# Casts of q and k with the heads outermost, four of them joined, and a new order of the first quarter of an attention-and-MLP kernel

## The chip, the core and the metric

The kernel runs on one core of a Trainium2 chip. A core has five engines that run beside each other, each with its own instruction queue taken strictly in the order in which the kernel wrote it: TensorE (PE in the profile; PEld is its weight load), VectorE (DVE), ScalarE (ACT), GpSimd (POOL) and SyncE (SP, which issues DMA transfers). An engine waits on semaphores for the others, and while it waits everything behind the waiting instruction in its queue waits too. The metric is the device time of one execution in microseconds (us), median of several runs.

## The reference

Four batches, eight heads, 768 positions, head size 64. Three of the heads are "retrieval" heads (0, 2, 6) with plain causal attention; the other five are "streaming" heads that see 4 sink positions and a window of 64. The attention output, 3072 tokens of 512, then goes through a two-layer MLP with a gate, 512 to 2048 to 512.

```python
scores = scale * np.matmul(q, k.transpose(0, 1, 3, 2))
full_mask = causal                        # retrieval heads
stream_mask = causal & (is_sink | in_win) # streaming heads
a = softmax(where(mask, scores, -1e9))
x = (a @ v).transpose(0, 2, 1, 3).reshape(B * S, H * D)
h = x @ w_in
g = h * (1 / (1 + exp(-beta * h)))
return g @ w_out
```

## The kernel before

**Tiling.** The 768 positions of a batch are two halves of 384, so there are 8 chunks (batch, half). A chunk has 4 units, each a pair of heads that share one 128-row tile; there are 32 units. The first two chunks, units 0 to 7, are the "first quarter".

**What a unit of the first quarter needs.** `load_qk` (line 107) loads q and k of a chunk as float32 in two groups `s0` and `s1` of four heads: units 0 and 1 read the one, units 2 and 3 the other. `cast` (240) turns one unit's q or k into bfloat16 (`qkb`, 128 rows by 384). `transpose_qk` (317) lets PE transpose it, three 128-column products into a PSUM bank `mm`, and `copy_qk` (325) brings it back to SBUF as `KT` or `QTD`. `sinks_of` (302) copies the keys that streaming heads use twice (`KO`). A unit's scores come as two tiles, 0 and 1. For each, `begin` (411) adds the mask with a product of an identity (line 422; unit 5 is masked afterwards on DVE instead, by `mask`, 472), `rows` (425) multiplies queries by keys (line 451) and `soft` (454) takes the exponential on ACT, 128 by 768 or 128 by 512 (line 460). The score tile `sp` has two buffers, so a third tile begins only when the first has been read by its exponential. `steps_PV` (515) multiplies by the values (line 532), `normalize` (538) divides on DVE, and for each pair of units `steps_X` (563) transposes the result with six products (line 570), which `copy_x` (578) copies to `xT`.

**The MLP.** `steps_G1` (592) makes 16 tiles `fi` of a chunk's hidden layer, four products of 384 columns each (line 600), a tanh on ACT (605) and a gate on DVE (608). `steps_G2` (624) is the second layer (line 653) and the output. A G1 tile of chunk 0 needs `xT` of both pairs of units and its quarter of `w_in`, which `load_w_in` (138) brings through POOL's DMA queue, as `load_w_out` (142) brings `w_out`.

**What sets the order.** Everything is recorded in a list written by hand. `RAMP` (785) covers units 0 to 7, `PLAN` (803) the other 24 units; each word is one step, and `do` (697) turns it into instructions. The order of the words gives each engine its own order; words for different engines don't wait for each other but for their data. The words that matter here, with `u` a unit and `i` a tile:

- `cku`, `cqu` casts of k and q, with the engine as last letter (`v` DVE, `a` ACT, `g` POOL); `tku`, `tqu` the transposes; `kku`, `kqu` the copies back; `kou` the sink keys.
- `adu.i`, `qku.i`, `exu.i` the mask product, the scores and the exponential; `pvu` two of the six parts of a unit's value product; `nou` the division; `mau.i` the mask of unit 5.
- `xxg`, `cxg` the transposes of a pair's output and its copy.
- `lvc.t`, `lqc.g` loads of v and of q and k, `win`, `won` of the weights, `cvc.t` the cast of v, `voc` copies of sink values. A `g` behind a load holds it back until POOL has reached that place.
- `zzn` issues n products of zeros, 512 columns each, whose result nobody reads (`keep_busy`, 510); nine more come at the very start (`idle`, 164).
- `mm`, `mA`, `mb` the next step of the MLP, `hm` and `hf` the two halves of a first G1 tile.

From `PLAN` on, PE always has MLP work to put between the steps of attention.

Of the kernel before, what the change touches and what calls it, by code (L numbers as in the profile page):

```python
# [10 lines left out]
F32 = mybir.dt.float32  # L11
# [7 lines left out]
def kernel(  # L19
# [13 lines left out]
    nc = tc.nc  # L33
# [68 lines left out]

    staged = {}
# [125 lines left out]
    def masks_late(h2):  # L231

        m = Mh[h2]
        if h2 == 0:
            return [lambda: nc.vector.tensor_copy(out=m[:, 3:5], in_=m[:, 1:3])]
        return [lambda i=i: nc.vector.tensor_copy(out=m[:, i:i + 2 * HT - 1:2], in_=Mh[0][:, i + 1:i + 2].to_broadcast([128, HT, 128]))
                for i in range(2)]


    def cast(u, name, copy):  # L240
        b, h2, p = units[u]
        c = u // NPAIR
        s = st_u.setdefault(u, {})
        if "qkb" not in s:
            s["qkb"] = att.tile([128, 2, HT, 2, D], BF16, name="qkb", bufs=4)
        copy(out=s["qkb"][:, "qk".index(name)], in_=staged[name, c, p // 2][:, p % 2:4:2].rearrange("p h t d -> p t h d"))
# [40 lines left out]
    def transposes_dma(c, names=("k", "q")):  # L287
# [10 lines left out]
        for u in range(c * NPAIR, (c + 1) * NPAIR):  # L298
            p = u % NPAIR
            st_u[u] = {"QT": QT[:, place[p], :]}  # L300

    def sinks_of(u):
# [12 lines left out]
        copy(out=ko[:, ka - 1:kz - 1, 0:64], in_=kt[:, None, 0:64].to_broadcast([128, n, 64]))  # L315

    def transpose_qk(u, name):

        s = st_u.setdefault(u, {})
        tp = ps_m.tile([128, 512], F32, name="mm").bitcast(BF16)[:, 0:HALF].rearrange("p (t j) -> p t j", t=HT)  # L320
        for t in range(HT):
            nc.tensor.transpose(tp[:, t, :], s["qkb"][:, "qk".index(name), t].rearrange("p h d -> p (h d)"), ident)  # L322
# [59 lines left out]
    def steps_QK(u):  # L382
# [89 lines left out]
        def mask(i):  # L472
            ev = views[i]
            ms = [[x for x, e in enumerate(tiles[i][r]) if e[5] is not None] for r in range(2)]
            if ms[0] and ms[0] == ms[1]:
                n = len(ms[0])
                m0 = tiles[i][0][0][5]
                nc.vector.tensor_mul(ev[:, :, 0:n], ev[:, :, 0:n], Mh[h2][:, None, m0:m0 + n].to_broadcast([128, 2, n, 128]))  # L478
            else:
                for r in range(2):  # L480
                    if ms[r]:
                        n = len(set(tiles[i][r][x][5] for x in ms[r]))
                        m0 = tiles[i][r][0][5]
# [213 lines left out]
    def do(word):  # L697
# [2 lines left out]
        n, i = int(n or 0), int(i or 0)  # L700
        if what in ("ck", "cq"):
            cast(n, what[1], copies[eng])
        elif what in ("tk", "tq"):
            step((170, lambda: transpose_qk(n, what[1])))
        elif what in ("kk", "kq"):
# [3 lines left out]
        elif what in ("ad", "qk", "ex", "ma"):  # L709
            if n not in visits:  # L710
                visits[n] = steps_QK(n)
            step((0 if what in ("ex", "ma") else 170, lambda: visits[n][what](i)))
        elif what == "cv":
            cast_v(n, i, copies[eng])
        elif what == "vo":
# [1 line left out]
        elif what == "pv":  # L717
            pv = products.setdefault(n, [])
            if not pv:
                pv.extend(steps_PV(n))  # L720
            run(pv[:2])
            del pv[:2]
        elif what == "no":
            normalize(n)
        elif what == "xd":
            x_by_dma(n)
        elif what == "xx":
            run(steps_X(n))
        elif what == "cx":
            copy_x(n, copies[eng])  # L730
        elif what == "on":
            ones_v(engines[eng], n)
        elif what == "ne":
            negatives([(0, 1, 2), (3, 4)][n])
        elif what == "be":
            step((100, beta_go))
        elif what == "lv":
            load_v(n, held=eng == "g", tiles=[i])
        elif what == "lq":
            load_qk(n, i, held=eng == "g")  # L740
        elif what == "wi":
            load_w_in(n)
        elif what == "wo":
            load_w_out(n)
        elif what == "rq":
            rows_queries()
        elif what == "rk":
            rows_keys()
        elif what == "ro":
            if n not in more_rows:  # L750
                more_rows[n] = load_rows(n)
            more_rows[n].pop(0)()
        elif what in ("dk", "dq"):
            transposes_dma(n, what[1])
        elif what == "ml":
            late[n].pop(0)()
# [12 lines left out]

    def feed(x):  # L770
# [141 lines left out]
```

## Time and profile before

| What | Value |
|---|---|
| median of 3 runs | 228.81 us (228.60 to 228.89) |
| profiled execution: span from first to last instruction | 227.0 us |
| what the median has beside that span | 1.8 us |
| PE busy | 219.4 us, 97% of the span |
| ACT busy | 154.0 us, 68% |
| DVE busy | 142.1 us, 63% |
| POOL busy | 87.3 us, 38% |
| mean granted TensorE clock | 0.999 |

No time of the profiled execution other than its span is given, so the median stands for it; the 1.8 us lie before the first and after the last instruction. In rows of the timeline the first number is the start in us from the start of the span, the second the length from the first start to the last end of a group of `x` instructions; then engine, line, operation, and output `<-` input. In brackets stands the idle time of the engine before the group, and what ended it. A product's row holds its latency too, so the next product starts before the row ends. "Busy" PE counts the products of zeros like any other.

### The profile page before, as it was taken

How to read it: one execution, taken by the hardware profiler on the slowest of the kernel's cores; microseconds unless marked ns; L12 is line 12 of the kernel's file. 1: busy time of each engine (PE TensorE's matmuls, PEld its weight loads, DVE VectorE, ACT ScalarE, POOL GpSimd, SP SyncE). 2: the span in 40 equal slices, each digit the busy share in tenths (PEclk: the TensorE clock that was granted, in tenths of full speed). 3: DMA queues.
4: the chain of work that ended last, by engine and by line, in shares of the span. 5: the costliest groups of instructions: out<-in, count | busy, mean ns of one | idle time of the engine just before them, and what ended most of it. 6: DMA issues, size and time to landing. Idle time of an engine off the chain costs nothing.

```text
span 227.0 us, 5019 instructions
## 1 busy us (share of the span) xinstructions
PE 219.4 (97%) x1898; PEld 126.4 (56%) x1917; DVE 142.1 (63%) x342; ACT 154.0 (68%) x254; POOL 87.3 (38%) x143
## 2 busy tenths in 40 slices
PE   7989999999999999999999999999999999999994
PEld 3555766654655665556654664556645655456553
DVE  4679888852684779357932699646963779028600
ACT  2698898946767897449933887569876878139621
POOL 5377952249163399143064049910670000000000
PEclk9999999999999999999999999999999999999999
DMA  6999999999999899989869779596963030111012
GB/s 204 262 301 239 225 197 198 195 220 171 149 216 178 161 153 144 141 175 133 103 131 162 126 151 140 92 133 103 216 64 107 24 81 0 49 46 46 0 49 92
DMA packets 95383, 31.66 MB, mean 139 GB/s; under 512 B 81776, under 2 KB 92416, under 8 KB 95360
## 3 DMA queue, kind: packets, MB, share of 16 engines
q1 hardware_dynamic: 58880, 22.82, 50.2%
q0 software_dynamic: 35904, 8.13, 41.9%
q10 hardware_dynamic: 576, 0.40, 0.6%
q8 instruction: 15, 0.25, 0.5%
q14 instruction: 8, 0.07, 0.1%
HBM read 27.27 MB, written 6.29 MB: 148 GB/s over the span
## 4 chain that ended last, share of the span: by engine, by line
PE 89%; DMA 4%; DVE 2%; SPq 2%; issue 1%; ACT 0%; ACTq 0%; DVEq 0%
PE mm L653 34%; PE mm L600 25%; PE sp L600 12%; PE sp L451 6%; PE po L532 6%; DMA s<-in_k_dram 3%; DMA s<-in_q_dram 2%; PE mm L638 2%; DVE es L478 1%; PE mm L322 1%; SPq L132 1%; PE mm L570 1%; PE mm L451 1%; SPq L119 1%; PE sp L422 1%
## 5 line engine op out<-in xcount | busy, mean ns | idle before, releaser
L653 PE MATMUL mm<-w_out_sb,gT 128*128 128x512 bf16 x349 | 84.1, 379 | 1.3 <-issue 0.5
L460 ACT ACTIVATE es<-sp 128x768 bf16<-128x768 f32 (+2 forms) x72 | 56.5, 837 | 19.6 <-PE sp L451 19.4
L600 PE MATMUL mm<-xT,w_in_sb 128*128 128x384 bf16 x348 | 64.6, 326 | 0.0
L600 PEld LDWEIGHTS <-w_in_sb 128*128 128x128 bf16 x512 | 47.8, 98 | 29.7 <-issue 0.2
L605 ACT ACTIVATE th<-mm,beta_h 128x384 f32<-128x384 f32 x87 | 49.8, 588 | 5.6 <-PE mm L600 0.9
L653 PEld LDWEIGHTS <-gT 128*128 128x128 bf16 x368 | 33.4, 98 | 36.0 <-issue 1.5
L608 DVE SCALAR_TENSOR_TENSOR gT<-th,mm 128x384 bf16<-128x384 f32 x87 | 46.8, 551 | 7.4 <-ACT th L605 3.8
L282 POOL DMA_DIRECT2D s<-in_q_dram x30 | 22.4, 761 | 27.2 <-DMA QTD<-s 21.7
L600 PE MATMUL sp<-xT,w_in_sb 128*128 128x384 bf16 x164 | 32.3, 326 | 0.0
L657 ACT ACTIVATE osb<-mm 128x512 f32<-128x512 f32 x23 | 13.8, 602 | 26.1 <-PE mm L653 25.8
L532 PEld LDWEIGHTS <-es 128*128 128x128 bf16 x472 | 23.3, 98 | 13.6 <-issue 1.5
L608 DVE SCALAR_TENSOR_TENSOR gT<-th,sp 128x384 bf16<-128x384 f32 x41 | 22.3, 552 | 5.6 <-ACT th L605 3.7
L532 PE MATMUL po<-VX,es 128*128 128x65 bf16 x360 | 24.9, 194 | 0.8 <-ACT VX L251 0.4
L605 ACT ACTIVATE th<-sp,beta_h 128x384 f32<-128x384 f32 x41 | 23.8, 586 | 2.3 <-PE sp L600 0.2
L282 POOL DMA_DIRECT2D s<-in_k_dram x30 | 22.4, 759 | 6.8 <-DMA w_out_sb<-in_moe_w_out_dram 5.2
L251 POOL CAST VX<-vs 128x512 bf16<-128x512 f32 x16 | 10.6, 662 | 34.6 <-DMA vs<-in_v_dram 31.8
L541 DVE RECIPROCAL rec<-po 128x6 f32<-128x6 f32 x28 | 5.4, 193 | 27.0 <-PE po L532 27.0
L478 DVE TENSOR_TENSOR es<-es,Mh 128x768 bf16<-128x768 bf16 (+1 forms) x26 | 17.4, 698 | 5.0 <-ACT es L460 4.4
L451 PE MATMUL sp<-QTD,KT 64*128 64x128 bf16 (+2 forms) x258 | 19.2, 240 | 0.6 <-ACT QTD L333 0.3
L545 DVE TENSOR_TENSOR x<-po,rec 128x384 bf16<-128x384 f32 x28 | 15.6, 557 | 1.0
L451 PEld LDWEIGHTS <-KT 64*128 64x128 bf16 x278 | 11.1, 94 | 5.8 <-issue 3.6
L259 POOL COPY VO<-VX 128x512 bf16<-128x512 bf16 x16 | 10.0, 649 | 7.3 <-DVE VX L251 7.3
(74 smaller groups left out, 157.2 us busy)
## 6 DMA issues: line engine op xcount, KB each, us to landing
vs<-in_v_dram SPq DMA_DIRECT2D x24, 256.0 KB, 5.5
out_dram<-osb SPq DMA_DIRECT2D x23, 256.0 KB, 2.8
w_in_sb<-in_moe_w_in_dram POOLq DMA_DIRECT2D x4, 512.0 KB, 9.7
w_out_sb<-in_moe_w_out_dram POOLq DMA_DIRECT2D x4, 512.0 KB, 16.5
s<-in_k_dram POOLq DMA_DIRECT2D x30, 64.0 KB, 4.8
s<-in_q_dram POOLq DMA_DIRECT2D x30, 64.0 KB, 5.1
s<-in_k_dram SPq DMA_DIRECT2D x4, 384.0 KB, 6.8
s<-in_q_dram SPq DMA_DIRECT2D x4, 384.0 KB, 8.6
```

What stands on the lines that cost most here:

```text
L251: copy(out=VX[b % 2][:, h2 * HT + t, :, 0:D], in_=staged["v", c][:, t])
L282: nc.gpsimd.dma_start(out=ROWS[c % 2, name][:, t, i * 4 * D:(i + 1) * 4 * D].rearrange("p (h d) -> p h d", d=D), in_=src[b, i:H:2, r:r + 1 ...
L451: nc.tensor.matmul(sps[i][r][:, x * 128:y * 128], key(a, lhs), s["QT"][half(a), qi * 128:(qi + y - x) * 128], start=first, stop=first or y ...
L460: nc.scalar.activation(out=views[i].rearrange("p r k j -> p r (k j)"), in_=banks[2][:, :, 0:n * 128], func=ACTF.Exp, scale=scale)
L478: nc.vector.tensor_mul(ev[:, :, 0:n], ev[:, :, 0:n], Mh[h2][:, None, m0:m0 + n].to_broadcast([128, 2, n, 128]))
L532: nc.tensor.matmul(po[:, qi, hh, :], e, val, start=(j == 0), stop=(j == len(lst) - 1))
L545: nc.vector.tensor_mul(xg[g][:, :, :, u % 2, :].rearrange("p a t d -> p t a d"), po[:, :, :, 0:D], rec.to_broadcast([128, HT, 2, D]))
L600: nc.tensor.matmul(hp[:, 0:HALF], w_in_sb[:, mo, fi * 128:(fi + 1) * 128], xT[c][:, mo, :], start=(mo == 0), stop=(mo == MO - 1))
L605: nc.scalar.activation(out=th, in_=hp[:, 0:HALF], func=ACTF.Tanh, scale=beta_h[:, fi:fi + 1])
L608: nc.vector.scalar_tensor_tensor(out=gTs[c][:, fi, :], in0=th, scalar=1.0, in1=hp[:, 0:HALF], op0=ALU.add, op1=ALU.mult)
L653: nc.tensor.matmul(op, gTs[c][:, fi, ns * 128:(ns + 1) * 128], w_out_sb[:, fi, :], start=(fi == 0), stop=(fi == FO - 1))
L657: nc.scalar.activation(out=osb, in_=op, func=ACTF.Copy, scale=0.5)
```

## The change

Three things are changed together.

First, `cast` reads and writes the same elements in another order of loops: the two heads of a unit outermost and the three tiles of 128 positions inside, instead of the other way round. In `qkb`, k now lies ahead of q.

Second, a new `cast_both` does k and q of one unit in one instruction of 128 by 768 (word `cbu`). It is used for units 0 (DVE), 2, 5 and 7 (POOL).

Third, `RAMP` is written anew. The work is the same except that there are 24 products of zeros instead of 9 (besides the nine at the start), five of them ahead of unit 0's first transposes, five and then four more ahead of its first scores. Casts and copies change engines: ACT loses all its casts of the ramp and has `kk0`, `kq1`, `kk2`, `kk3` and `cx0`; DVE loses `ck3`, `ck6`, `cq5` and `cx0` and has casts of v; POOL has `ck3`, `ck6` and the three wide casts. The loads `lq1.0` and `lv3.0` are no longer held back by POOL, and `lq2.1` now is; `wi3` comes behind `wo0`. `mA` stands in two places for `mm` (the tile goes to the other PSUM pool). From `PLAN` on the order is the same on every engine.

`mask` and `masks_late` take the engine as an argument, which the words still set to DVE. `transpose_two` and `copy_two` are new and no word calls them.

```diff
     def load_qk(c, g, pairs=1, held=False):
...
         both = stage.tile([128, 2, 4, HT, D], F32, name=f"s{g}")
+        both_of[c, g] = both
...
             s["qkb"] = att.tile([128, 2, HT, 2, D], BF16, name="qkb", bufs=4)
-        copy(out=s["qkb"][:, "qk".index(name)], in_=staged[name, c, p // 2][:, p % 2:4:2].rearrange("p h t d -> p t h d"))
+        copy(out=s["qkb"][:, "kq".index(name)].rearrange("p t h d -> p h t d"), in_=staged[name, c, p // 2][:, p % 2:4:2])
...
+    def cast_both(u, copy):
+        c, p = u // NPAIR, u % NPAIR
+        s = st_u.setdefault(u, {})
+        s["qkb"] = att.tile([128, 2, HT, 2, D], BF16, name="qkb", bufs=4)
+        copy(out=s["qkb"].rearrange("p i t h d -> p i h t d"), in_=both_of[c, p // 2][:, :, p % 2:4:2])
...
     RAMP = """
-        ck0g ne1 lv0.0 lv0.1 tk0 ck2a ne0 cq0v ck1a zz3 tq0 kq0a zz3 ad0.0 on0v lv0.2 kk0v cq1v tq1 qk0.0 tk2 ad0.1
-        kq1v tk1 kk1v lq1.0g be qk0.1 ex0.0 zz3 ad1.0 cv0.0g ko1 lq1.1 ex0.1 pv0 ck3v cq3g tk3 lv1.0g cq2a tq2 kk3v
-        lv1.1 cv0.1g ad1.1 qk1.1 kk2v ex1.1 tq3 ko2 qk1.0 wi0 vo0 cq4g lv1.2 cv0.2a lq2.0g ko3 pv0 kq2v pv0 ad2.0
-        qk2.0 lv2.0 ex1.0 pv1 kq3a pv1 ck4v ad2.1 qk2.1 lv2.1 pv1 ex2.0 ad3.0 tq4 no0 tk4 ex2.1 ck7g kk4a qk3.0 ad3.1
-        qk3.1 no1 pv2 ck6v ex3.0 cq5v ck5g pv2 tk6 xx0 ad4.0 cq6g pv3 kq4v ex3.1 pv2 ad4.1 cx0v ad5.0 qk4.1 pv3 lv2.2
-        no2 on1g tq5 pv3 qk4.0 kk6a ml0 tk5 cq7g kq5v ex4.1 kk5a ko5 ko6 ad5.1 tq6 wi1 qk5.0 ex4.0 tk7 tq7 ex5.0 no3
-        qk5.1 ex5.1 kq6v xx1 ad6.0 kk7v wi2 kq7v wi3 cx1a qk6.0 ml1 ad6.1 ex6.0 cv1.1g ko7 qk6.1 cv1.0v ex6.1 hm lq2.1
-        ma5.0 ma5.1 mm cv1.2g vo1 mm wo0 pv4 lv3.0g ad7.0 lv3.1 pv4 hf pv4 no4 qk7.0 ad7.1 pv5 pv5 ex7.0 lv3.2 qk7.1
-        pv5 no5 ml1 wo1 ex7.1 pv6 pv6 wo2 mm pv7 rq pv7 pv7 no7 wo3 pv6 no6 rk cq8g xx2 ro3 cx2a mA mA ck8g xx3 cx3a
...
+        cb2g zz1 zz1 cb0v zz1 ne1 ck1v zz1 cq1v zz1 tq0 lv0.0 ad0.0 ad0.1 zz5 tk0 tk1 be lv0.1 zz3 ck3g zz1 ne0 kq0a
+        lv0.2 tq1 kk1v lq1.0 kk0a kq1a qk0.0 ko1 ex0.0 qk0.1 lq1.1 zz1 cq3g ex0.1 tk2 cv0.1g zz3 ad1.0 kk2a lv1.0g
+        ad1.1 zz1 cv0.0v zz2 lv1.1 tq2 lv1.2 tk3 wi0 qk1.1 qk1.0 ex1.1 kq2v ko2 vo0 zz3 cq4g kk3a ad2.0 on0v tq3 ko3
+        pv0 cv0.2v pv0 lv2.0 qk2.0 ex1.0 ad2.1 ck6g kq3v pv0 pv1 ex2.0 pv1 qk2.1 ck4v ad3.0 pv1 ex2.1 cb5g tq4 tk4
+        pv2 qk3.0 ad3.1 lq2.0g pv2 no0 kk4a kq4v ex3.0 qk3.1 no1 tk6 lv2.1 pv2 kk6v cb7g ex3.1 xx0 pv3 pv3 cx0a
+        ad4.0 ad4.1 qk4.1 ex4.1 no2 tk5 ad5.0 pv3 tq5 kk5a cq6v lv2.2 qk4.0 ad5.1 kq5v tq6 ko5 ex4.0 ko6 on1g qk5.0
+        tk7 wi1 lq2.1g qk5.1 no3 kq6v xx1 ex5.0 ex5.1 wi2 tq7 rk cx1a ad6.0 hm ad6.1 kk7v kq7v qk6.0 qk6.1 cv1.1g
+        ex6.0 mm cv1.0v ko7 mlv ma5.v pv4 ma5.1 ml1 cv1.2v pv4 ex6.1 ad7.0 mm lv3.0 pv4 vo1 hf no4 wo0 ad7.1 wi3
+        qk7.0 pv5 lv3.1 qk7.1 pv6 pv5 wo1 pv5 ex7.0 pv6 wo2 ex7.1 mm no5 ml1 pv6 pv7 pv7 no6 pv7 xx2 wo3 cq8g rq
+        lv3.2 cx2a no7 mA mA xx3 cx3a ro3 mm mA mm mA mm mA mm mA mm mA mm mm mm mA ro3 ro3 mm mA ro3 mm mm ck8g mA
...
     """
```

More of the change, by code (lines that the diff above doesn't have):

```diff
@@ L300, in transposes_dma, with transpose_two, copy_two @@
             st_u[u] = {"QT": QT[:, place[p], :]}
+    def cast_both(u, copy):
[3 more added lines that the diff above has]
+        copy(out=s["qkb"].rearrange("p i t h d -> p i h t d"), in_=both_of[c, p // 2][:, :, p % 2:4:2])
+    def transpose_two(u, name):
+        tp = ps_m.tile([128, 512], F32, name="mm").bitcast(BF16)[:, 0:2 * HALF].rearrange("p (u t j) -> p u t j", u=2, t=HT)
+        for i in range(2):
+            for t in range(HT):
+                nc.tensor.transpose(tp[:, i, t, :], st_u[u + i]["qkb"][:, "kq".index(name), t].rearrange("p h d -> p (h d)"), ident)
+        two_tp[u, name] = tp
+    def copy_two(u, name, copy):
+        b, h2, p = units[u]
+        tp = two_tp.pop((u, name)).rearrange("p u t j -> p u j t")
+        if name == "k":
+            copy(out=KTB[b % 2][:, place[p]:place[p + 1] + 1:place[p + 1] - place[p], h2 * HALF:(h2 + 1) * HALF].rearrange("p u (j t) -> p u j t", t=HT), in_=tp)
+        else:
+            for i in range(2):
+                st_u[u + i]["QT"] = QTB[(u + i) % 3]
+            copy(out=QTD[1][:, u % 3:u % 3 + 2, :].rearrange("p u (j t) -> p u j t", t=HT), in_=tp)
+    two_tp = {}
     def sinks_of(u):
@@ L321, in transpose_qk @@
         for t in range(HT):
-            nc.tensor.transpose(tp[:, t, :], s["qkb"][:, "qk".index(name), t].rearrange("p h d -> p (h d)"), ident)
+            nc.tensor.transpose(tp[:, t, :], s["qkb"][:, "kq".index(name), t].rearrange("p h d -> p (h d)"), ident)
         s["t" + name] = tp
@@ L470, in visit, with mask @@
             return (56 * sum(len(tiles[i][0]) for i in some) + 250, go)
-        def mask(i):
+        def mask(i, eng=nc.vector):
             ev = views[i]
@@ L702, in do @@
             cast(n, what[1], copies[eng])
+        elif what == "cb":
+            cast_both(n, copies[eng])
+        elif what in ("wk", "wq"):
+            step((340, lambda: transpose_two(n, what[1])))
+        elif what in ("yk", "yq"):
+            copy_two(n, what[1], copies[eng])
         elif what in ("tk", "tq"):
@@ L711, in do @@
                 visits[n] = steps_QK(n)
-            step((0 if what in ("ex", "ma") else 170, lambda: visits[n][what](i)))
+            if what == "ma":
+                step((0, lambda: visits[n][what](i, engines[eng or "v"])))
+            else:
+                step((0 if what == "ex" else 170, lambda: visits[n][what](i)))
         elif what == "cv":
@@ L755, in do @@
         elif what == "ml":
-            late[n].pop(0)()
+            late[n].pop(0)(copies[eng or "v"])
         elif what == "tt":
@@ L797 @@
+        mm mA mm ro3 mm mm ro3 mA mA mb mb tt8 mb mb mb
     """
```

16 lines of the change are left out of this document (7 added, 9 removed).

## The prediction

> **What bounds the kernel now.** I read the table of stages first, cut where PE's work changes character: 5.13 us (warm products begin), 7.40 (first scores), 17.43 (first scores of chunk 1), 29.30 (both chunks' `xT` are there), 223.74 (last product).
>
> ```profile
> core 0: us, PE busy (x) PEld busy (x) DVE busy (x) ACT busy (x) POOL busy (x), PEclk, DMA share, GB/s
> 7.40:17.43 10.03, 9.33 (x124) 5.63 (x124) 6.87 (x17) 7.67 (x13) 6.78 (x19) 1.00 1.21 271
> 17.43:29.30 11.87, 11.61 (x155) 7.69 (x154) 10.88 (x27) 10.36 (x17) 8.90 (x17) 1.00 1.21 231
> 29.30:223.74 194.44, 192.74 (x1597) 110.56 (x1614) 120.55 (x288) 132.94 (x219) 68.40 (x94) 1.00 0.92 125
> ```
>
> After 29.30 PE idles 1.7 of 194.4 us, and its order there doesn't change. Whatever the ramp loses or wins up to the last transposes of `xx3` therefore moves the end by as much. Then the chain of waits, for the ramp's limits and for a rate:
>
> ```profile
> 9.35 5.93 DMA s<-in_k_dram
> ...
> 15.84 0.54 DVE qkb L246
> 16.39 0.48 DVE QTD L333
> ...
> 29.95 0.65 PE sp L600 x4
> ```
>
> The ramp before waits for the second half of chunk 1's k (landed at 15.28), then for casts on DVE. The last row gives PE's warm rate: 4 x 384 columns in 0.65 us, 0.423 ns a column; a product of 512 zeros costs 0.217. Last the timeline, for what each step takes:
>
> ```profile
> 1.29 3.83 PE L167 MATMUL mm<-zeros 128*128 128x512 bf16 x9 [1.29 <-DVE zeros L157]
> 4.29 0.51 POOL L246 CAST qkb<-s 128x384 bf16<-128x384 f32 x1
> 4.93 0.53 DVE L246 CAST qkb<-s 128x384 bf16<-128x384 f32 x1
> 4.96 0.33 PE L322 MATMUL mm<-idb,qkb 128*128 128x128 bf16 x3
> 5.13 0.81 PE L513 MATMUL po<-zeros 128*128 128x512 bf16 x3
> ...
> 6.88 0.47 ACT L333 COPY QTD<-mm 128x384 bf16<-128x384 bf16 x1
> 7.40 0.34 PE L451 MATMUL sp<-QTD,KT 64*128 64x128 bf16 x4 [0.34 <-ACT QTD L333]
> 7.78 0.81 ACT L460 ACTIVATE es<-sp 128x768 bf16<-128x768 f32 x1 [0.43 <-PE sp L451]
> 8.88 0.81 ACT L460 ACTIVATE es<-sp 128x768 bf16<-128x768 f32 x1 [0.29 <-PE sp L451]
> ...
> 10.96 0.60 ACT L460 ACTIVATE es<-sp 128x512 bf16<-128x512 f32 x1 [0.88 <-PE sp L451]
> ...
> 13.03 1.53 ACT L460 ACTIVATE es<-sp 128x768 bf16<-128x768 f32 x2
> ...
> 15.42 1.31 ACT L460 ACTIVATE es<-sp 128x768 bf16<-128x768 f32 x2
> ...
> 17.81 0.81 ACT L460 ACTIVATE es<-sp 128x768 bf16<-128x768 f32 x1 [0.71 <-PE sp L451]
> 18.87 0.48 ACT L330 COPY KT<-mm 128x384 bf16<-128x384 bf16 x1 [0.25 <-PE mm L322]
> 19.25 2.01 ACT L460 ACTIVATE es<-sp 128x768 bf16<-128x768 f32 x3
> 21.12 0.83 ACT L579 COPY xT<-mm 128x768 bf16<-128x768 bf16 x1
> 21.80 1.57 ACT L460 ACTIVATE es<-sp 128x768 bf16<-128x768 f32 x2
> ```
>
> The reader is to see two things. Unit 0's casts find their data at 4.29 and 4.93 without waiting, so its load is no limit. And ACT's exponentials run from 7.78 almost without a break; `ex4.1` at 17.81 is the one that waited, for scores whose queries stood on DVE behind the casts that the late k held up.
>
> **The sum, step by step.** *First scores.* The three transposes that follow the nine cold products begin at 4.96. In the new order PE issues from there to `qk0.0`: fourteen products of zeros (7168 columns), `tq0`, `tk0`, `tk1`, `tq1` (1536), unit 0's masks (768) and `be` (16), 9488 columns x 0.423 ns = 4.0 us. So `qk0.0` can't start before 9.0; before it started at 7.40. PE's order is strict, so the 3.0 us of zeros are paid in full where unit 0 would have been ready: its wide cast on DVE, begun by 4.3, is two of the 0.53 us casts at most, over by 5.4, while `tq0` stands behind five products at 6.0.
>
> *First exponentials.* `tq1` ends issuing at 9.0, its result is there 0.17 later (0.33 for three, of which 0.16 are issue). ACT has `kq1` ahead of `ex0.0` now: 9.2 + 0.48, so `ex0.0` runs 9.7 to 10.5 and `ex0.1` to 11.3. `ad1.1` needs the second score buffer back, 11.3. Behind it PE has the mask (512 columns, 0.22), three zeros (0.65), `tq2`, `tk3` (0.33) and `qk1.1` (0.22): 12.8, and with the latency `ex1.1` starts at 12.95. Before it was 10.96. **The ramp is 2.0 us late here.** The three zeros ahead of `ad1.0` and the single one cost nothing, the wait for `ex0.0` covers them.
>
> *From `ex1.1` to `ex4.1`.* ACT's queue holds `ex1.1` 0.60, `kk3` 0.48, `ex1.0` 0.81, `ex2.0` and `ex2.1` 1.53, `kk4` 0.48, unit 3's two 1.31, `cx0` 0.83: 6.0 us. Without any idle time `ex4.1` starts at 19.0, against 17.81: 1.2 late. So 0.8 are won back, because nothing waits for the late k any more: `ck6` is on POOL and DVE's `kq4` is free of it. But I don't take ACT without idle time. `qk2.1` stands on PE behind `ad2.1` (free when `ex1.0` ends, 14.8) and three `pv` steps: mask 0.22, twelve 65-column products 0.33, scores 0.32, latency 0.17, which makes 1.05 us where `ex2.0` covers 0.8. I take 0.4 for this and the like place at unit 3 (`qk3.0` behind mask, `tq4`, `tk4` and two `pv`, 1.3 us, covered by `ex2.1` and `kk4`, 1.25) together: 1.6 late.
>
> *From there to `xx3`.* `ex4.1` 0.81, `kk5` 0.48, three exponentials 2.01, `cx1` 0.83, then unit 6, a tanh between each pair and unit 7, as before. Before there was one gap of 0.25 (18.87), now there is one of about 0.35, `qk5.0` behind `kk5` with scores and latency. So 1.7 late at `ex7.1`, and PE, which then has the same products left, at `xx3`. Ends: 1.0 (ACT never idle from `ex1.1` on, the old gap of 0.25 saved as well) and 2.7 (a gap of 0.35 at three more places where scores stand behind masks and `pv`, at units 3, 4 and 6).
>
> *DVE, casts.* Rows on either side of what isn't in the trace, a cast with heads outermost:
>
> ```profile
> 58.69 0.55 DVE L246 CAST qkb<-s 128x384 bf16<-128x384 f32 x1
> 59.15 0.42 DVE L251 CAST VX<-vs 128x512 bf16<-128x512 f32 x1
> ```
>
> 512 elements in 0.42 beside 384 in 0.55: the order of loops can cost more than the elements. The wide cast lies between 0.42 (of a 512) and 1.1; either way it is over before `tq0`, so it counts zero, cover: the five zeros. Four other casts on DVE in the ramp may each give 0.2 back, and the three that leave for POOL 1.6; DVE gets v casts at 0.42 for it. It has slack in all of 7.40 to 17.43 (6.87 of 10.03), so zero; after 17.43 it is nearly full (10.88 of 11.87), and `cx0` leaving it is a cover for the rest. [...]
>
> *POOL.* Wide casts are not in the trace: between 0.65 (512 elements, below) and two of 0.51. I take 1.0. `cb2` starts when q of unit 2 lands, about 6.6, ends by 7.6 and is wanted by `tk2` at 9.6. `cb5` and `cb7`:
>
> ```profile
> 16.66 0.51 POOL L246 CAST qkb<-s 128x384 bf16<-128x384 f32 x1 [0.30 <-DMA s<-in_q_dram]
> ...
> 22.09 0.65 POOL L251 CAST VX<-vs 128x512 bf16<-128x512 f32 x1
> ...
> 22.90 0.83 POOL L251 CAST VX<-vs 128x512 bf16<-128x512 f32 x1
> ```
>
> `ck6` to 15.9, `cb5` to 16.9, `cb7` to 17.9; first wanted by `tk5` at 19.3. Zero, with 1.4 us to spare. [...]
>
> *SP and loads.* The order of loads up to `lv1.2` is the same and SP reaches `lq1.0` after POOL had released it anyway; `lv1.0` is released after `cv0.1` at about 11 instead of 10.4. First use of that v: `pv4`, past 24. Zero. `lv2.0` ahead of `lq2.0` and the later `lq2.1` feed chunk 2, `cq8` at the earliest: zero.
>
> *Weights.* This is the one move with little room:
>
> ```profile
> 19.89 2.23 POOL L140 DMA_DIRECT2D w_in_sb<-in_moe_w_in_dram  x3
> ...
> 34.37 0.75 POOL L282 DMA_DIRECT2D s<-in_k_dram  x1 [1.55 <-DMA w_in_sb<-in_moe_w_in_dram]
> 37.76 0.74 POOL L282 DMA_DIRECT2D s<-in_k_dram  x1 [2.64 <-DMA w_out_sb<-in_moe_w_out_dram]
> ```
>
> ```profile
> 29.14 0.81 PE L600 MATMUL mm<-xT,w_in_sb 128*128 128x384 bf16 x4
> ```
>
> POOL's transfers land one every 3.4 us, `wi3` at 34.3, `wo0` at 37.7. Swapped, `wi3` lands at 37.7 plus what `wi1` starts later (behind `ko5`, `ko6`, `on1`: up to 1.7), 39.4. It is wanted by the 21st G1 tile: six are issued before 29.14, so 29.14 + 14 x 0.65 = 38.2, plus 1.7 = 39.9. It is hidden by 0.5 us; zero.
>
> **Sum.** Span 227.0 + 1.7 = 228.7; with the 1.8 us that the median of the runs has beside this span, 230.5. No time of the profiled execution other than its span is given, so nothing else is corrected.
>
> **Rivals.** *Faster: the ramp was never bound by its early tiles.* DVE's wait for the late k ends at 15.28; the new order takes it out of DVE's queue, and then all that counts is PE's own work. Both orders issue the same 42,700 columns up to `xx3` (counted in the instruction lists). Without any wait the new one is through at 4.96 + 42,700 x 0.423 ns (18.1) + 24 x 0.217 (5.2) = 28.3 instead of 29.14: 0.9 faster, 227.9. It decides if `ex4.1` starts before 17.0. Against it: `ad1.1` waits for `ex0.1` whatever else happens, and ACT's queue gives 19.0 at best.
>
> *No change: the late data hide it.* If chunk 1's units wait for loads anyway, the 2.0 us are absorbed. For: the chain before runs through the load. Against: by ACT's own queue the new order comes to unit 4 at 19.0, 3.7 us behind that landing, so no load is left there to hide in. Time: 228.8.
>
> *Much slower: `wi3` comes too late.* If more than the 0.5 us is lost, the whole MLP waits, up to one landing of 3.4 less the 0.5: 1 us takes it to 231.5, all of it to 233.4.
>
> [...]
>
> **How the numbers follow.** Late by the step count 0.60 (with either cast time); late and `wi3` too 0.10; absorbed 0.09; faster 0.21. A measurement of this kernel can tell about 0.2%, 0.5 us. The likeliest case alone spans 229.8 to 231.5 (1.0 to 2.7 late). To hold 8 in 10 I reach down to 228.3, into the faster case, and up to 231.8. Chances: faster 0.21, within 0.2% 0.09, slower 0.70.
>
> **What would show it.** `qk0.0` at 9.0 or later, `ex0.0` near 9.7, `ex1.1` near 12.95, `ex4.1` between 19 and 19.7; the last `xx3` transposes near 30.8 instead of 29. Casts: 0.34 to 0.55 for 384 on DVE. PE without a gap at the 21st G1 tile. Wrong would be: the first scores earlier than PE's order allows by my count, or `ex4.1` before 18.

## The result, and the profile after

The changed kernel takes 231.69 us (median of 6 runs, 230.33 to 232.16) against 228.70 for the kernel before in the same series (6 runs, 228.02 to 229.46). The ratio is 1.0115 with a 95% interval of 1.0079 to 1.0151: slower by 1.8 to 3.5 us. The profiled execution took 231.93 us, its span is 230.2, against 227.0 before. In the runs below, 231.90 (no24) and 233.75 (after_oldcasts) are slow executions, over 1.5% above the fastest of their kernel: medians and ranges count them, ratios leave them out.

First the table of stages of the changed kernel, cut at the same events as before: first scores, first scores of chunk 1, both chunks' `xT` there, last products.

```profile
core 0: us, PE busy (x) PEld busy (x) DVE busy (x) ACT busy (x) POOL busy (x), PEclk, DMA share, GB/s
9.97:19.48 9.51, 9.25 (x129) 6.36 (x128) 5.03 (x15) 7.66 (x13) 6.68 (x15) 1.00 1.15 269
19.48:32.16 12.68, 11.27 (x150) 7.52 (x150) 11.95 (x28) 10.88 (x18) 10.30 (x20) 1.00 1.16 226
32.16:226.86 194.70, 192.90 (x1598) 110.52 (x1614) 120.59 (x288) 132.94 (x219) 66.39 (x91) 1.00 0.91 122
```

The start takes 2.6 us more (9.97 against 7.40), the middle 0.5 less (9.51 against 10.03), the stage of chunk 1 0.8 more (12.68 against 11.87), with PE idle for 1.4 us of it and DVE busy for 11.95, and the last stage 0.3 more (194.70 against 194.44).

Then the timeline of the changed kernel: start, length, engine, line, output `<-` input.

```profile
1.29 4.02 PE L168 MATMUL mm<-zeros 128*128 128x512 bf16 x9 [1.29 <-DVE zeros L158]
5.11 1.72 PE L539 MATMUL po<-zeros 128*128 128x512 bf16 x5
6.66 0.33 PE L348 MATMUL mm<-idb,qkb 128*128 128x128 bf16 x3
...
9.71 0.33 PE L348 MATMUL mm<-idb,qkb 128*128 128x128 bf16 x3
9.97 0.51 PE L477 MATMUL sp<-QTD,KT 64*128 64x128 bf16 x10
10.45 1.52 ACT L486 ACTIVATE es<-sp 128x768 bf16<-128x768 f32 x2
13.64 0.60 ACT L486 ACTIVATE es<-sp 128x512 bf16<-128x512 f32 x1 [1.30 <-PE sp L477]
19.87 0.81 ACT L486 ACTIVATE es<-sp 128x768 bf16<-128x768 f32 x1
...
23.25 0.63 POOL L252 CAST VX<-vs 128x512 bf16<-128x512 f32 x1
23.31 0.87 DVE L252 CAST VX<-vs 128x512 bf16<-128x512 f32 x1
23.80 0.52 POOL L338 COPY KO<-KT 128x128 bf16<-128x128 bf16 x1
23.94 0.81 ACT L486 ACTIVATE es<-sp 128x768 bf16<-128x768 f32 x1 [0.21 <-PE sp L477]
24.09 0.87 DVE L236 COPY Mh<-Mh 128x256 bf16<-128x256 bf16 x1
24.27 0.61 POOL L260 COPY VO<-VX 128x512 bf16<-128x512 bf16 x1
24.88 1.29 DVE L504 TENSOR_TENSOR es<-es,Mh 128x768 bf16<-128x768 bf16 x2
26.30 0.58 DVE L252 CAST VX<-vs 128x512 bf16<-128x512 f32 x1
26.94 0.31 PE L558 MATMUL po<-VX,es 128*128 128x65 bf16 x5 [0.97 <-DVE VX L252]
28.10 1.30 ACT L486 ACTIVATE es<-sp 128x768 bf16<-128x768 f32 x2
32.00 0.81 PE L626 MATMUL mm<-xT,w_in_sb 128*128 128x384 bf16 x4
```

Four places are to be seen. `qk0.0` starts at 9.97, 2.57 late. `ex1.1` starts at 13.64 behind a wait of 1.30, 2.68 late. `ex4.1` at 19.87 is 2.06 late, so 0.6 is won back in between. And the value products of unit 4 (line 558) wait 0.97 for a cast of v on DVE; unit 7's exponentials come at 28.10 (before 25.15) and the first G1 products behind `xx3` at 32.00 (before 29.14), both 2.9 late. What is left after that is 198.2 us of the span, against 197.9.

Last the groups of casts of the changed kernel, by form (count, then busy us and mean ns of one).

```profile
L247 DVE CAST qkb<-s 128x384 bf16<-128x384 f32 x7 | 2.6, 380 | 0.8 <-DMA s<-in_k_dram 0.8
L307 POOL CAST qkb<-s 128x768 bf16<-128x768 f32 x3 | 2.5, 820 | 2.8 <-DMA s<-in_q_dram 2.8
```

A cast of 384 on DVE took 0.38 (0.55 in the row shown of before), and POOL's wide cast of 768 took 0.82.

### The profile page after: what moved, and what is told of

Same layout as the page of the kernel before. It is cut to its first block, busy times and chain, and to the rows that moved or that the text cites. A ratio compares the mean times of both kernels' runs of the same rounds, so it can differ in the third digit from the quotient of the medians.

```text
span 230.2 us, 5040 instructions
## 1 busy us (share of the span) xinstructions
PE 222.1 (96%) x1912; PEld 128.4 (56%) x1932; DVE 141.1 (61%) x341; ACT 154.2 (67%) x253; POOL 87.4 (38%) x140
## 4 chain that ended last, share of the span: by engine, by line
PE 90%; DVE 4%; DMA 3%; issue 1%; ACT 1%; ACTq 0%
PE mm L679 31%; PE mm L626 23%; PE sp L626 12%; PE po L558 6%; PE sp L477 6%; DMA xT<-x 3%; PE po L539 2%; PE mm L348 2%; PE mm L168 2%; PE mm L664 2%; DVE es L504 1%; PE sp L448 1%; PE mm L596 1%; PE mm L477 1%; ACT es L486 1%
## 5 line engine op out<-in xcount | busy, mean ns | idle before, releaser
L631 ACT ACTIVATE th<-mm,beta_h 128x384 f32<-128x384 f32 x85 | 48.5, 587 | 6.4 <-PE mm L626 1.6
L634 DVE SCALAR_TENSOR_TENSOR gT<-th,mm 128x384 bf16<-128x384 f32 x85 | 45.6, 551 | 6.8 <-ACT th L631 3.2
L626 PE MATMUL sp<-xT,w_in_sb 128*128 128x384 bf16 x172 | 33.9, 326 | 0.0
L634 DVE SCALAR_TENSOR_TENSOR gT<-th,sp 128x384 bf16<-128x384 f32 x43 | 23.4, 552 | 5.8 <-ACT th L631 3.6
L631 ACT ACTIVATE th<-sp,beta_h 128x384 f32<-128x384 f32 x43 | 24.9, 585 | 2.4 <-PE sp L626 0.2
L252 POOL CAST VX<-vs 128x512 bf16<-128x512 f32 x14 | 8.8, 627 | 29.9 <-DMA vs<-in_v_dram 28.3
L477 PE MATMUL sp<-QTD,KT 64*128 64x128 bf16 (+2 forms) x258 | 18.7, 240 | 0.0
```

Source lines behind the costliest of these rows:

```text
L477: nc.tensor.matmul(sps[i][r][:, x * 128:y * 128], key(a, lhs), s["QT"][half(a), qi * 128:(qi + y - x) * 128], start=first, stop=first or y ...
L626: nc.tensor.matmul(hp[:, 0:HALF], w_in_sb[:, mo, fi * 128:(fi + 1) * 128], xT[c][:, mo, :], start=(mo == 0), stop=(mo == MO - 1))
L631: nc.scalar.activation(out=th, in_=hp[:, 0:HALF], func=ACTF.Tanh, scale=beta_h[:, fi:fi + 1])
L634: nc.vector.scalar_tensor_tensor(out=gTs[c][:, fi, :], in0=th, scalar=1.0, in1=hp[:, 0:HALF], op0=ALU.add, op1=ALU.mult)
```

## The experiments

Diffs show only the words of `RAMP` that differ. All ratios are to the kernel before, measured beside each run.

**The 14 early products of zeros taken out** (run no14).

```diff
-        cb2g zz1 zz1 cb0v zz1 ne1 ck1v zz1 cq1v zz1 tq0 lv0.0 ad0.0 ad0.1 zz5 tk0 tk1 be lv0.1 zz3 ck3g zz1 ne0 kq0a
+        cb2g cb0v ne1 ck1v cq1v tq0 lv0.0 ad0.0 ad0.1 tk0 tk1 be lv0.1 ck3g ne0 kq0a
```

> The changed kernel without the fourteen products of zeros ahead of the first scores (words zz1 x5, zz5, zz3, zz1 before qk0.0); the other ten stay. Theory (the zeros stand in PE's strict queue and delay unit 0): first scores move from 9.97 to about 6.8 us, the first exponential from 10.45 to about 7.3, ex4.1 from 19.87 to between 16.8 and 17.5 (q of unit 4 lands at 14.2), the wait of 1.0 us for the v cast stays; about 2.5 us less than the changed kernel, 229.2. Rival 1 (the zeros bring PE to its full clock, products of 512 columns took 0.43 us until about 5.9 us): the transposes and scores up to 8.5 us run at half rate, the gain is 1 us or less, 230.7. Rival 2 (late loads and the moved casts make the ramp late): no change, 231.7.

Measured: 228.43 us (12 runs, 228.19 to 229.22), ratio 0.9990 [0.9976, 1.0003]. The whole loss is gone, 0.8 us more than the theory expected. The timeline of this run:

```profile
7.87 1.52 ACT L486 ACTIVATE es<-sp 128x768 bf16<-128x768 f32 x2
11.07 0.60 ACT L486 ACTIVATE es<-sp 128x512 bf16<-128x512 f32 x1 [1.30 <-PE sp L477]
14.50 0.50 POOL L247 CAST qkb<-s 128x384 bf16<-128x384 f32 x1 [0.92 <-DMA s<-in_q_dram]
15.06 0.51 PE L348 MATMUL mm<-idb,qkb 128*128 128x128 bf16 x6 [0.69 <-POOL qkb L247]
18.16 0.81 ACT L486 ACTIVATE es<-sp 128x768 bf16<-128x768 f32 x1
29.85 0.81 PE L626 MATMUL mm<-xT,w_in_sb 128*128 128x384 bf16 x4
```

Against the changed kernel the exponentials come 2.6 us earlier at units 0 and 1, but only 1.7 at `ex4.1`: POOL's cast of unit 4's q now waits 0.9 us for its load and starts at 14.50, and PE waits 0.7 us for the cast. The rest of the first quarter starts from there and ends at 29.85, 2.15 earlier than with the zeros.

**Zeros put into the kernel before** (before_8_zeros), eight products ahead of its `qk0.0`:

```diff
-... zz3 ad0.0 on0v lv0.2 kk0v cq1v tq1 qk0.0 tk2 ad0.1
+... zz3 ad0.0 on0v lv0.2 kk0v cq1v tq1 zz8 qk0.0 tk2 ad0.1
```

> The kernel before with eight more products of zeros just ahead of its first scores (word zz8 before qk0.0), nothing else: 8 x 0.217 = 1.7 us of PE, of which 0.34 falls into a wait that was there, so unit 0's scores come 1.4 us later. Theory (early tiles bind only in part; before chunk 1 ACT idles 0.5 us at 14.6 and 0.7 at 17.1, which can take up a delay): 0.2 to 0.9 us slower, 229.2. Rival 1 (every early us of PE is paid at the end): 1.4 slower, 230.0. Rival 2 (the load of chunk 1 hides all that happens before it): no change, 228.6.

Measured: 230.50 us (6 runs, 229.86 to 231.03), ratio 1.0067 [1.0042, 1.0092], 1.0 to 2.1 us. Eight warm products are 8 x 0.217 = 1.7 us. The theory missed; the first rival's 1.4 lies in the interval. In the timeline of this run:

```profile
7.86 1.89 PE L513 MATMUL po<-zeros 128*128 128x512 bf16 x8
9.69 0.34 PE L451 MATMUL sp<-QTD,KT 64*128 64x128 bf16 x4
10.06 0.81 ACT L460 ACTIVATE es<-sp 128x768 bf16<-128x768 f32 x1 [2.45 <-PE sp L451]
31.14 0.81 PE L600 MATMUL mm<-xT,w_in_sb 128*128 128x384 bf16 x4
```

The first scores start 2.29 late and the products behind `xx3`, at 31.14, 2.0 late. Part of this is not the eight zeros: PE came up to its full rate later here than in the profile of before, where the three zeros behind the first transposes took 0.81 us; here they took 1.49. They took 1.49 as well in the profile of before_heads (below), which has no further zeros, and there the first scores start at 8.05 and the products behind `xx3` at 29.35. Against that profile the eight zeros cost 1.64 and 1.79. So zeros ahead of the first scores are paid in full in the old order too.

**All 24 taken out** (no24).

```diff
-... zz1 cb0v zz1 ... zz5 tk0 ... qk0.1 lq1.1 zz1 cq3g ex0.1 tk2 cv0.1g zz3 ad1.0 ... ad1.1 zz1 cv0.0v zz2 ... vo0 zz3 cq4g
+... cb0v ... tk0 ... qk0.1 lq1.1 cq3g ex0.1 tk2 cv0.1g ad1.0 ... ad1.1 cv0.0v ... vo0 cq4g
```

> The changed kernel without any of the 24 products of zeros in its ramp. Theory (of the ten left without the fourteen, the three behind ad1.1 and the three ahead of ad2.0 stand in the path of the exponentials, the other four in a wait; but q of unit 4 lands at 14.2 and POOL's cast of it is waited for by 0.7 us already): the exponentials of unit 1 come 0.6 us sooner, unit 4's at most 0.2, the time within 0.3 us of that without the fourteen, 228.3. Rival 1 (all six count): 1.3 us less, 227.1. Rival 2 (gaps on PE bring its clock down): 0.5 us or more slower, products of 128 columns at 0.107 instead of 0.055 us apart somewhere between 6 and 16 us.

Measured: 228.57 us (12 runs, 227.91 to 231.90), ratio 0.9998 [0.9979, 1.0017], the same as without 14. PE's waits in this run (total us, times, longest):

```profile
PE mm L348 <- POOL qkb L247: 1.3, 1, 1.3
PE mm L348 <- POOL qkb L307: 1.0, 1, 1.0
PE po L558 <- DVE VX L252: 1.0, 2, 0.6
```

`ex1.1` came at 9.79, 1.3 earlier than without the 14, and PE spent the gain at 15.74, waiting 1.3 us for POOL's cast of unit 4's q, whose load is late (0.7 in no14). The wait of 1.0 is for unit 2's wide cast, at 8.24. The ten later zeros cost nothing: without them PE idles there. Nor were the 24 needed to keep PE at its full rate, as the second rival had it: six transposes take 0.51 us at 15.74, behind the longest wait, and 0.50 elsewhere.

**The new order of loops alone** (before_heads), in the kernel before:

```diff
-        copy(out=s["qkb"][:, "qk".index(name)], in_=staged[name, c, p // 2][:, p % 2:4:2].rearrange("p h t d -> p t h d"))
+        copy(out=s["qkb"][:, "qk".index(name)].rearrange("p t h d -> p h t d"), in_=staged[name, c, p // 2][:, p % 2:4:2])
```

> The kernel before with the new order of loops in its casts alone (two heads outermost), nothing else. Theory (casts lie off the path that sets the end): a DVE cast of 384 falls from 0.54 to about 0.35 us as in the changed kernel, POOL's and ACT's stay near 0.5, the time stays within 0.3 us of 228.7. Rival 1 (DVE is nearly full from 17 to 29 us, so cheaper casts shorten the ramp): 0.5 to 1 us faster. Rival 2 (the faster mode of DVE holds up POOL's casts): POOL's casts longer by 0.1 to 0.3 us, 0.3 us or more slower.

Measured: 228.58 us (12 runs, 228.24 to 229.77), ratio 1.0004 [0.9990, 1.0018]. The nine casts on DVE fell from a mean of 543 to 430 ns, those on POOL stayed (524 and 535). Nothing waits for the 0.1 us.

**The old order of loops in the new order of work** (after_oldcasts), each wide cast as two of 384:

```diff
-        copy(out=s["qkb"].rearrange("p i t h d -> p i h t d"), in_=both_of[c, p // 2][:, :, p % 2:4:2])
+        for i in range(2):
+            copy(out=s["qkb"][:, i], in_=both_of[c, p // 2][:, i, p % 2:4:2].rearrange("p h t d -> p t h d"))
```

> The changed kernel's order, with the casts of q and k in the old order of loops (tiles outermost, heads inside) and each wide cast as two instructions of 384. It asks what the cast form is worth inside the new order. Theory, nothing: DVE's casts go back from 0.35 to 0.54 us and the first unit's takes 1.0 instead of 0.8, all of it covered by the products of zeros and by ACT's queue; POOL's pairs take 1.03 instead of 0.82 against 1.4 us to spare: 231.4 to 232.0 us, like the changed kernel's 231.69. Rival, the new order needs the faster casts: the casts of unit 5 and 7 on POOL come late for their transposes, or DVE's last casts push the cast of v tile 2 back further: 232.3 us or more.

Measured: 231.19 us (7 runs, 230.22 to 233.75), ratio 1.0093 [1.0058, 1.0129], the same as the changed kernel within the intervals. DVE's seven casts were back at 544 ns and the wait of PE for v was 1.0 as before. The form of the casts, wide or not, is worth nothing measurable in either order.

**The cast that PE waits for moved to POOL** (`cv1.2g`), in the changed kernel (cv12_pool) and then without the 14 zeros (no14_cv12_pool):

```diff
-... ma5.v pv4 ma5.1 ml1 cv1.2v pv4 ...
+... ma5.v pv4 ma5.1 ml1 cv1.2g pv4 ...
```

> The changed kernel with one word changed, the cast of the last v tile of chunk 1 back on POOL (cv1.2g for cv1.2v). Theory (in the changed kernel PE waits 0.97 us at 25.97 for this cast, which stands on DVE behind the masks of unit 5): the wait is gone, 0.8 us less, 230.9. Rival (the cast is late because v is, or POOL gets as full as DVE and the weights' transfers behind it come later): no change or slower, 231.7 to 232.5.

Measured: 231.52 us (6 runs, 230.91 to 233.71), ratio 1.0134 [1.0102, 1.0167]: nothing gained, the theory missed. PE now waits 0.8 us for the first cast of v, which stayed on DVE. The timeline of this run says why:

```profile
22.87 0.63 POOL L252 CAST VX<-vs 128x512 bf16<-128x512 f32 x1
22.93 2.19 DVE L252 CAST VX<-vs 128x512 bf16<-128x512 f32 x1
23.42 0.31 POOL L338 COPY KO<-KT 128x128 bf16<-128x128 bf16 x1
23.66 0.62 POOL L252 CAST VX<-vs 128x512 bf16<-128x512 f32 x1
24.22 0.62 POOL L260 COPY VO<-VX 128x512 bf16<-128x512 bf16 x1
25.04 0.21 DVE L236 COPY Mh<-Mh 128x256 bf16<-128x256 bf16 x1
```

One DVE cast of 512, begun 0.06 us behind a cast on POOL, lasted as long as POOL had one element operation after the other, and ended some 0.3 us after them.

> Both edits: no zeros ahead of the first scores, and cv1.2 on POOL. Theory: the two terms add, 2.5 + 0.8 us less than the changed kernel, 228.4, about level with the kernel before or a little faster. Rival (the second wait only showed because everything was late; with the zeros gone the masks of unit 5 are done earlier): no better than without the zeros alone, 229.2.

Measured: 228.55 us (12 runs, 228.04 to 230.68), ratio 1.0008 [0.9988, 1.0029], like no14. Here POOL stood waiting for the load of v up to 21.90, DVE's cast ran alone at 21.07 in 0.42, and PE had no wait for v left. The products behind `xx3` start at 28.82 instead of 29.85, and yet the median is no better. The theory's number came out, but not by its sum: the second term added nothing.

**The first cast of v on ACT** as well (cv10_act_cv12_pool):

```diff
-... mm cv1.0v ko7 ... ml1 cv1.2v pv4 ...
+... mm cv1.0a ko7 ... ml1 cv1.2g pv4 ...
```

> The changed kernel with all its zeros, cv1.2 on POOL as in cv12_pool and cv1.0 on ACT instead of DVE. In cv12_pool a v cast of 512 on DVE (cv1.0) took 2.19 us from 22.93 on, beside an unbroken run of POOL instructions from 22.14 to 24.84, where the same form takes 0.42 elsewhere; PE waited 0.81 us for it. Theory (DVE's cast was held up by POOL, and that wait took the place of the one removed): with the cast on ACT, 0.61 us of it, PE doesn't wait ahead of pv4 and the time falls 0.5 to 0.8 us below that of the changed kernel, 231.0. Rival 1 (v itself lands late): the wait stays, 231.6. Rival 2 (ACT is the limit there, its 0.61 us are paid): 231.6 to 232.

Measured: 231.72 us (6 runs, 231.08 to 234.05), ratio 1.0111 [1.0082, 1.0140]. Nothing gained, the theory missed: PE waited 1.2 us for the same cast, now on ACT, and 1.5 us for `w_in` at 32.6. The profiled execution took 234.05 us, so only the places of the waits are read from it.

**POOL's cast of v one place earlier**, so that POOL issues a transfer while DVE casts, in the changed kernel (cv11_early) and without the 14 zeros (no14_cv11_early):

```diff
-... ex5.0 ex5.1 wi2 tq7 rk cx1a ad6.0 ... qk6.1 cv1.1g ex6.0 ...
+... ex5.0 ex5.1 cv1.1g wi2 tq7 rk cx1a ad6.0 ... qk6.1 ex6.0 ...
```

> The changed kernel, with one word moved on POOL: the cast of v tile 1 of chunk 1 stands between the second and third w_in transfer instead of behind the third, so that POOL issues a transfer (0.75 us) while DVE makes its cast of v tile 0. Theory, POOL's element work stretches DVE's copies: in the changed kernel that DVE cast took 0.87 us and the mask copy behind it 0.87, beside POOL busy without a break, against 0.42 and 0.22 in the run without early zeros and with the cast of tile 2 on POOL. With POOL issuing transfers there instead, the cast goes back to about 0.42, the mask copy to 0.2 to 0.5, the cast of tile 2 starts near 25.4 instead of 26.30, and PE's wait for it shrinks from 1.0 to 0.3 us or less: 230.9 to 231.2 us. Rival, DVE's own queue is too long whatever POOL does: the cast stays at 0.87 or the wait at 1.0, time 231.5 to 231.9. Against both: the third w_in transfer starts 0.55 us later; if its quarter is missed, slower than 232.

Measured: 231.20 us (6 runs, 230.28 to 232.93), ratio 1.0107 [1.0062, 1.0153]. In size neither expectation is decided, for the interval covers both. In mechanism the theory hit half: the mask copy was back at 0.30, but the cast took 0.79, beside the issue of a transfer on POOL and the copy of sink keys behind it, and PE still waited 0.8.

> The changed kernel without the 14 products of zeros ahead of the first scores, and with the cast of v tile 1 of chunk 1 one place earlier on POOL as in the other run of this call. Without the 14 zeros alone PE waited 0.6 us for the cast of v tile 2 on DVE, 0.7 for POOL's cast of q or k, 0.4 for the division, and the time was 228.43. Theory, the first of these is POOL's doing and lies on the path: it goes, 227.8 to 228.0 us, faster than before by 0.3%. Rival, the versions without early zeros all end at 228.5 because the loads of chunk 1 pace them: another wait of the same size takes its place (v tile 1 not yet landed when POOL comes to it, or the w_in transfer behind it), 228.3 to 228.6.

Measured: 229.66 us (12 runs, 228.88 to 230.81), ratio 1.0040 [1.0015, 1.0065]: a miss for both expectations, it is slower. PE's wait for v did go, and the first quarter ended at 28.83. The timeline of this run shows what came instead:

```profile
28.83 0.81 PE L626 MATMUL mm<-xT,w_in_sb 128*128 128x384 bf16 x4
38.57 0.82 PE L626 MATMUL mm<-xT,w_in_sb 128*128 128x384 bf16 x4 [0.48 <-DMA w_in_sb<-in_moe_w_in_dram]
49.76 3.61 PE L679 MATMUL mm<-w_out_sb,gT 128*128 128x512 bf16 x16 [0.29 <-DMA w_out_sb<-in_moe_w_out_dram]
```

The last quarters of both weights come too late, 0.8 us together; most of the 1.0 us won ahead of `xx3` is lost there. That explains why nothing was gained. This execution took 229.18; why the median lies 0.9 us above the kernel before is not shown.

**No zeros, and transposes put where their data are ready** (no24_reordered; `cv1.2g` too):

```diff
-... ad1.0 kk2a lv1.0g ad1.1 ... tq2 lv1.2 tk3 ... cb5g tq4 tk4 pv2 ... no0 kk4a kq4v ex3.0 qk3.1 no1 tk6 ...
+... ad1.0 kk2a lv1.0g tq2 tk3 ad1.1 ... lv1.2 ... cb5g pv2 ... no0 ex3.0 qk3.1 no1 tq4 tk4 kk4a kq4v tk6 ...
```

> The changed kernel without zeros, with cv1.2 on POOL, tq2 and tk3 ahead of ad1.1 (into the wait for the second exponential) and tq4, tk4, kk4 and kq4 behind the scores of unit 3, so that the late q of unit 4 holds up nothing of unit 3. Theory (what is left in the ramp are waits of PE of 0.7 us for POOL's cast of q of unit 4 and the gap of 1.3 us in ACT ahead of ex1.1): unit 3's exponentials begin by 14.2 instead of 15.98 (without the fourteen), but from unit 4 on the loads set the pace (k of units 6 and 7 lands at 15.3): 0.3 to 0.8 us faster than the kernel before, 228.1. Rival 1 (the loads set everything from unit 4 on): no faster than without the fourteen, 228.4. Rival 2 (the order is paced by ACT alone): 1.5 us faster, 227.1.

Measured: 228.46 us (12 runs, 228.12 to 228.79), ratio 0.9988 [0.9974, 1.0001]. `ex1.1` at 9.72 and `ex4.1` at 17.52, the products behind `xx3` at 28.64, 0.5 earlier than in the kernel before, and then a wait of 0.3 us for `w_in` at 38.2. In time it is the first rival.

**The same with `wi3` ahead of `wo0`** (reordered_wi3_first), as in the kernel before:

```diff
-... hf no4 wo0 ad7.1 wi3 qk7.0 ...
+... hf no4 wi3 ad7.1 wo0 qk7.0 ...
```

> The version without zeros and with the reordered transposes (cast of v tile 2 on POOL), with one more edit: the fourth w_in transfer ahead of the first w_out transfer on POOL, as in the kernel before. In that version the last transposes of the first quarter ended 0.5 us earlier than before (28.64 against 29.14), but PE then waited 0.3 us for the fourth quarter of w_in at 38.2; in the run with the early cast of v tile 1 it waited 0.5 there and 0.3 for w_out at 49.8. Theory, the arrival of the weights is part of what holds all versions at 228.5: the wait at 38.2 goes, w_out one landing later is still in time before 46, 228.0 to 228.2 us, ratio near 0.997. Rival, the weights only trade places: PE waits for w_out near 46 to 50 by as much, 228.4 to 228.6. Second rival, what is left after the first quarter varies by 0.5 us without any wait of PE (198.2, 197.9 and 197.4 us so far) and swallows it: 228.4 without a wait for either.

Measured: 228.43 us (11 runs, 228.16 to 228.99), ratio 0.9993 [0.9975, 1.0010]. The wait for `w_in` is gone, none for `w_out` takes its place, and the time doesn't change: the second rival. This order can't be told from the kernel before.

## Why the prediction was right, and where it was off

The forecast was 230.5 us, slower, with 229.8 to 231.5 for the likeliest case and 228.3 to 231.8 for 8 in 10; 231.69 lies just above the first and just inside the second. The mechanism is the one predicted: no14 takes the time back to that of before, and eight zeros in the old order cost what their columns cost. The size was off: 1.7 us late at `xx3` by the sum, 2.86 in the profile, 2.99 between the medians.

- *First scores*, at 9.0 or later: 9.97. The columns were right, their rate was not. The sum took all of them warm. In the changed kernel's profile the five zeros from 5.11 take 1.55 us up to the next product, where five warm ones take 1.08: about two were still cold, 0.5 us. Another 0.15 is the later end of the nine cold ones, the rest 0.3 lies in small gaps around `tk1`, `be` and `tq1`, 0.1 to 0.15 each. The point from which the products take their warm time differs between the profiles: before 4.96 in that of before, near 6.0 in that of after, and only near 7.0 in that of before_heads, where three transposes from 6.71 on still take 0.32 us up to the next product, against 0.17 from 4.96 on in before. That last profile has the same order of work as before, and its first scores are 0.65 later. Part of the missed half microsecond can therefore lie between two executions and not in the change; what sets the point is not shown.
- *First exponentials*: 10.45 and 13.64 instead of 9.7 and 12.95. Both are late by 0.7, less than the start's 0.97: from the first scores to `ex0.0` the sum took 0.7 us and the profile has 0.48. From there to `ex1.1` the steps were right, 3.25 by the sum and 3.19 in the profile.
- *From `ex1.1` to `ex4.1`*: 0.4 won back by the sum, 0.6 in the profile.
- *From there to `xx3`*: this is the step that failed. The sum had 0.1 more lost; the profile has 0.8, and PE waits 0.97 at one place, unit 4's value products behind `cv1.2` on DVE. It goes back to the step *DVE, casts*, "so zero; after 17.43 it is nearly full (10.88 of 11.87), and `cx0` leaving it is a cover for the rest". The cover was counted in busy time, but the durations themselves grew. From the start of `cv1.0` to that of `cv1.2` on DVE stand the cast, the mask copies and two masks of unit 5. That takes 2.0 us in no14_cv11_early, where POOL is waiting for a load up to 21.83, and PE has no wait for v:

```profile
20.99 0.42 DVE L252 CAST VX<-vs 128x512 bf16<-128x512 f32 x1
21.83 0.65 POOL L252 CAST VX<-vs 128x512 bf16<-128x512 f32 x1 [1.55 <-DMA vs<-in_v_dram]
22.99 0.82 DVE L252 CAST VX<-vs 128x512 bf16<-128x512 f32 x1
```

  It takes 2.8 in no14 and in cv11_early and 3.0 in the changed kernel, where POOL is at work beside it, and PE waits 0.6, 0.8 and 0.97. With 2.0 in the changed kernel `cv1.2` would start at 25.3 and, at its 0.58, be over by 25.9, when PE's wait begins. This is read from single executions: no run with the 14 zeros got rid of the wait, so its price in time is not measured.
- *Casts*: 0.34 to 0.55 for 384 on DVE were expected, the 0.34 as an estimate of the author; 0.38 was measured, and they counted zero rightly. The wide cast on DVE, put between 0.42 and 1.1, took 0.56 to 0.79 in the profiles, as the last section shows. The casts with the tiles outermost took 0.53 to 0.55.
- *POOL*: the wide casts took 0.82 (1.0 taken) and were hidden. What no step counts is that DVE's casts get longer beside POOL's work: 0.87 for a cast of v in the changed kernel, against 0.42 at 21.07 in no14_cv12_pool, while POOL waits.
- *Weights*: zero was right. But only just: with `wi3` behind `wo0` and `xx3` brought to 28.6 or 28.8, two of three versions wait for it (0.3 and 0.5 us), as the half microsecond of room said.
- *Rivals.* "Faster: PE's own work" needed `ex4.1` before 17.0; even without any zeros it is 17.4 at the earliest (reordered_wi3_first). "No change: the late data hide it" was wrong for the changed kernel, whose start is later than the loads, but it holds in part for the versions without zeros: 1.3 us won at `ex1.1` between no14 and no24 change nothing.

What stays open is the level itself. Five different orders of the first quarter without the early zeros all measure 228.4 to 228.6, like the kernel before; a sixth, no14_cv11_early, is slower. In their profiles the products behind `xx3` start between 28.64 and 30.52, but each profile is one execution: those of no24 (229.68) and no14 (229.02), where they start latest, took 1.1 and 0.6 us more than their medians. What is left behind that point varies too, though the order there is the same from `PLAN` on: 197.3 us in the profile of before_heads, 197.9 in that of before, 198.2 in that of the changed kernel. Waits for loads of chunk 1 (0.9 us on POOL in no14) and for weights (0.3 to 0.8 us on PE) take a part of the gains back, but with the waits for weights gone (reordered_wi3_first, 28.84, 0.3 earlier than before) the median still doesn't fall. A gain of 0.3 is no more than these variations; whether a smaller one is there stays open.

## What to carry to other kernels

Filler products meant to hold PE at its warm rate belong only where PE would wait anyway: ahead of the first scores, for which everything waited here, they cost their full columns (eight of them, 1.7 us by their columns, 1.64 at the first scores and 1.79 behind `xx3` in before_8_zeros against before_heads). What an edit wins at the start of a kernel can be lost at the next late load (the 1.3 us won at `ex1.1` between no14 and no24 ended in PE's wait of 1.3 us for a cast whose load is late), so find that load first. And before moving copies and casts between DVE and POOL, look at what the other one does in the same microsecond: free time on DVE was no room here, where its cast of 512 took 0.42 us while POOL waited, 0.87 beside a cast on POOL and once 2.19.

## What was not expected of the hardware

DVE's casts with the heads outermost, its casts of v and its mask copies took longer beside POOL's element work begun ahead of them than they took alone; its casts with the tiles outermost did not. In the kernel before, whose casts have the tiles outermost, two casts on each engine ran side by side, each DVE cast in 0.54 to 0.55 us (0.53 to 0.55 for all nine) and each of POOL's in 0.50 to 0.51; in before_heads, with the heads outermost, the same two on DVE took 0.57 and 0.65, against 0.35 at 19.75 in the changed kernel, where POOL is idle. The rows of before, then of before_heads:

```profile
15.37 1.01 DVE L246 CAST qkb<-s 128x384 bf16<-128x384 f32 x2 [0.49 <-DMA s<-in_k_dram]
15.40 0.96 POOL L246 CAST qkb<-s 128x384 bf16<-128x384 f32 x2 [0.66 <-PE sp L451]
```

```profile
15.31 1.08 POOL L246 CAST qkb<-s 128x384 bf16<-128x384 f32 x2 [0.18 <-PE mm L322]
15.45 1.15 DVE L246 CAST qkb<-s 128x384 bf16<-128x384 f32 x2
```

So the new order of loops gives a faster cast (0.35 us) that lost its gain beside POOL in before_heads (0.57 and 0.65).

The same cast of 512 took 0.42 us alone, 0.87 beside one POOL cast begun first, 2.19 beside four POOL operations in a row; the mask copy 0.22 alone and 0.87 beside POOL. It goes the other way too: in no14, where DVE's cast began at 21.60 and POOL's at 21.68, DVE's took 0.42 and POOL's 0.80 instead of 0.63. The two mask products of unit 5 (line 504), which read two inputs, are stretched as well: 0.89 in reordered_wi3_first, where POOL begins beside the last 0.2 us of them, 1.29 in the changed kernel and 1.71 in cv11_early. The wide cast shows it most plainly: in the ten profiles with it POOL ends an operation at 4.33 or 4.34, and the cast ends at 4.73 to 4.79 whether it begins at 3.94 or at 4.23.

```profile
3.92 0.41 POOL L188 TENSOR_SCALAR_AFFINE_SELECT Nc<-Nc 128x256 bf16<-128x256 bf16 x1
3.94 0.79 DVE L307 CAST qkb<-s 128x768 bf16<-128x768 f32 x1 [1.91 <-DMA s<-in_q_dram]
```

These are the timeline's rows of the changed kernel, where it begins at 3.94 and ends at 4.73; of the run without any zeros the row is this, with the end at 4.75:

```profile
4.17 0.58 DVE L307 CAST qkb<-s 128x768 bf16<-128x768 f32 x1 [2.13 <-DMA s<-in_q_dram]
```

So in these profiles the cast ended 0.40 to 0.46 us after POOL's operation, whenever it had begun. The 2.19 us, seen once, show more: behind the cast on POOL three further operations there ran their usual 0.31 to 0.62 us before the DVE cast ended. Why the two engines stretch each other's work is not shown by these runs.
